# A fused attention and FFN kernel: 256-column halves, two h tiles in one PSUM bank and one pass of 512 columns

## The chip, the cores and the metric

The kernel runs on one core of a Trainium2 chip. The metric is the device time of one execution in microseconds (us). The core has a matrix engine (PE, with its own queue of weight loads, PEld), a vector engine (DVE), a scalar engine (ACT), a general engine (POOL), and queues that issue DMAs (SP and ACT here). Each engine works through its instructions in an order fixed when the kernel is built. [...]

## What is computed

Attention for 8 batches, 8 heads, 576 positions and head size 64, followed by a feed-forward network (512 to 2048 to 512) over all 4608 rows:

```python
cum = np.cumsum(np.maximum(s, 0.0), axis=-1)
bias = -(cum[:, :, :, None] - cum[:, :, None, :])
scores = np.where(causal, -1e9, q @ k.T / sqrt(D) + np.minimum(bias, 0.0))
x = softmax(scores) @ v            # all heads side by side: 4608 x 512
h = x @ w_in                       # 4608 x 2048
g = np.where(h >= 1, h, np.where(h <= -1, 0.0, (h + 1) ** 2 / 4.0))
out = g @ w_out                    # 4608 x 512
```

## The kernel before

Everything is kept transposed: columns are positions, partitions are features. The 576 positions of a batch are cut into two halves (`HALF`): 320 columns (`hf` 0) and 256 columns (`hf` 1). An operand that needs more than fp16 is held as a high and a low fp16 part, so each product takes three matmuls (high-high, low-high, high-low).

**The FFN.** A half has 16 steps, one for each 128 of the 2048 hidden features (`ft` 0 to 15). In a step, `ffn_h` runs 12 matmuls (L530) that sum one h tile into one PSUM bank. The pool `ps_h` has two banks. The activation follows, on three engines in turn: ACT makes u from h (relu with scale and bias, L542), DVE combines h and u (L545), then clips and multiplies (L546), ACT casts the result to fp16 as the high part of g (L556), and POOL subtracts to get the low part (L557). The cast and the subtraction are not issued at once. They wait in `to_split`, and `g_split` issues them behind the relu of the next step (`issue_after(first)`), so that ACT does not stand waiting for DVE.

`ffn_y` runs the 12 matmuls (L569) of one step into four y tiles, one PSUM bank each (tags y0 to y3), that stay open over all 16 steps. At step 15 each y tile is scaled into an SBUF tile `o` (L583 on ACT, L581 on DVE for two tiles of the last half) and written out by DMA (L584). The o tiles take turns in three buffers, the u tiles in four, the g tiles (four steps each) in four.

**The order.** `ffn_step(s, k)` is called with k = 0 (h of step s) and k = 1 (y of an earlier step). y runs `Y_LAG` = 2 steps behind h, over the queue `ffn_q`. The first half of batch 0 is an exception: all 16 h come first, then all y, while the second weight matrix is being prepared.

**Attention beside it.** `att_slot` spreads the attention of the next batch over the same steps: scores on PE (L412, L413; L407 in the first jobs) into the two banks of `ps_s`, a masked minimum on DVE (L418), exp on ACT (L429), the scaled and split weights pb on POOL, ACT and DVE (L450 to L456), a transposing DMA (pt from pb), the product with v on PE (px, L475), and x from it (L486, L487). The 320-column half of the FFN and the 256-column half each have four (head pair, half) jobs of attention beside them, and the jobs need different amounts of work. The last batch's FFN has little or none beside it.

PSUM's eight banks are two of `ps_s`, two of `ps_h` and four of `ps_y`. Which instruction comes first on an engine is chosen by a planner when the kernel is built, from priorities in program order; `high_priority(offset=FFN_LEAD)` moves the activation of the FFN ahead of most attention work, and the masked minimum (`TTR_LEAD`) ahead of that.

Of the kernel before, what the change touches and what calls it, by code (L numbers as in the profile page):

```python
# [9 lines left out]
F32 = mybir.dt.float32  # L10
# [4 lines left out]
AF = mybir.ActivationFunctionType  # L15
ALU = mybir.AluOpType
# [14 lines left out]
HALF = [(0, 320, (0, 1, 2)), (320, 256, (3, 4))]  # L31
# [14 lines left out]
W2_LEAD = 6000  # L46

G_BUFS = 4
O_BUFS = 3
WO_LAG = 2  # L50

Y_LAG = 2

ACT_LOW = {'wi': range(0, 16, 2), 'wo': range(0, 16, 2)}
POOL_LO = {'wi': (8, 12, 13, 14, 15), 'wo': range(16)}
# [16 lines left out]
def attention_ffn(ctx: ExitStack, tc: tile.TileContext, qT, kT, vT, s, w_in, w_out, yT):  # L72
    nc = tc.nc
    LOADQ, CUMQ = nc.sync, nc.scalar
    V, A, G, T = nc.vector, nc.scalar, nc.gpsimd, nc.tensor
# [86 lines left out]
    WI = [cp.tile([P, 2, NC], F16, name=f"WI{c}") for c in range(NW)]  # L162
    WO = [cp.tile([P, 2, NC], F16, name=f"WO{c}") for c in range(NW + WO_LAG)]
# [4 lines left out]
    class Weights:  # L168
# [80 lines left out]
    vraw, csc, rcs, exs, hsc, rsc, usc, wsc, ubi, gsc, ysc, msc = ({} for _ in range(12))  # L249
# [268 lines left out]
            att_out(*jobs[j - 1])  # L518


    ffn_q, g4 = [], [None]

    def ffn_h(b, hf, ft):
        h_off, N, _ = HALF[hf]
        x = X[b, hf]
        h = ps_h.tile([P, 512], F32, tag="h", name=f"h{b}_{hf}_{ft}")
        n = 0
        for kt in range(NKT):
            for wl, xl in ((0, 0), (0, 1), (1, 0)):
                T.matmul(  # L530
                    h[:, :N], WI[4 * kt + ft // 4][:, wl, ft % 4 * P:(ft % 4 + 1) * P], x[:, kt, xl],
                    start=(n == 0), stop=(n == 3 * NKT - 1),
                )
                n += 1
        r, fg = rsc[b], ft // 4
        if ft % 4 == 0:
            g4[0] = gp.tile([P, 4, 2, N], F16, tag="g", bufs=G_BUFS, name=f"g{b}_{hf}_{ft}")
        g = g4[0][:, ft % 4]
        with tc.high_priority(offset=FFN_LEAD):

            u = gp.tile([P, N], F32, tag="u", bufs=4, name=f"u{b}_{hf}_{ft}")
            first = A.activation(u, h[:, :N], AF.Relu, bias=ubi[b], scale=usc[b][:, fg:fg + 1]).ins  # L542

            g_split(first)
            V.scalar_tensor_tensor(h[:, :N], h[:, :N], wsc[b][:, fg:fg + 1], u, ALU.mult, ALU.max)  # L545
            V.scalar_tensor_tensor(u, u, r, h[:, :N], ALU.min, ALU.mult)  # L546
        to_split.append((g, u))
        return g

    to_split = []  # L550

    def g_split(first=None):
        while to_split:
            g, u = to_split.pop()
            with tc.issue_after(first) if first is not None else ExitStack():
                A.copy(g[:, 0], u)  # L556
            G.tensor_tensor(g[:, 1], u, g[:, 0], ALU.subtract)  # L557

    ys = {}

    def ffn_y(b, hf, ft, g, ms=tuple(range(NKT))):
        h_off, N, _ = HALF[hf]
        if ft == 0:
            for m in ms:
                ys[b, hf, m] = ps_y.tile([P, 512], F32, tag=f"y{m}", name=f"y{b}_{hf}_{m}")
        for m in ms:
            c0 = ft % 2 * 2 * P + m % 2 * P
            for n, (wl, gl) in enumerate(((0, 0), (1, 0), (0, 1))):
                T.matmul(  # L569
                    ys[b, hf, m][:, :N], WO[8 * (m // 2) + ft // 2][:, wl, c0:c0 + P], g[:, gl],  # L570
                    start=(ft == 0 and n == 0), stop=(ft == NFT - 1 and n == 2),
                )
        if ft == NFT - 1:
            last = (b, hf) == (B - 1, len(HALF) - 1)
            for m in ms:
                tag, bufs = ("u", 4) if last and m >= 2 else ("o", O_BUFS)
                o = gp.tile([P, N], F32, tag=tag, bufs=bufs, name=f"o{b}_{hf}_{m}")
                y = ys[b, hf, m][:, :N]
                with tc.high_priority(offset=FFN_LEAD):
                    if last and m % 2:  # L580
                        V.tensor_scalar(o, y, ysc[b][m // 2], None, ALU.mult)  # L581
                    else:
                        A.activation(o, y, AF.Copy, scale=ysc[b][m // 2])  # L583
                (nc.sync if last and m % 2 else nc.scalar).dma_start(  # L584
                    yT[m * P:(m + 1) * P, b * S + h_off:b * S + h_off + N], o
                )

    def ffn_step(s, k):

        b, hf, ft = s // (2 * NFT), s // NFT % 2, s % NFT  # L590
        if k == 0:
            ffn_q.append((b, hf, ft, ffn_h(b, hf, ft)))
        elif len(ffn_q) > Y_LAG:
            ffn_y(*ffn_q.pop(0))


    for c in range(3):
# [4 lines left out]
    for j in range(NPAIR):  # L602
        for k in range(8):
            if k % 2 == 0:
                c = 4 * j + k // 2
# [55 lines left out]
    with tc.high_priority(offset=FFN_LEAD):  # L661
        g_split()
    while ffn_q:
        ffn_y(*ffn_q.pop(0))
# [28 lines left out]
```

## Time and profile before

| | |
|---|---|
| three runs | 1110.91, 1114.15, 1114.35 us; median 1114.15 |
| profiled execution | 1111.73 us, of which the span is 1109.9 us |
| mean granted PE clock over the span | 0.963 of full speed |
| h and y matmuls of 320 columns | 1536 each, busy 254.1 and 251.0 us |
| h and y matmuls of 256 columns | 1536 each, busy 209.8 and 206.8 us |
| output DMAs | 32 of 160 KB, 32 of 128 KB |

The span runs from the first instruction to the last; the 1.8 us beside it are around it. Busy time of PE counts a pipelined matmul until its modelled end, so a busy PE need not be at its peak; what is read from the profile is where PE is not busy, and on what it waits. In the rows of the groups, the columns are line, engine, operation, tiles written and read, shapes and count, then busy us in total, mean ns of one, and the idle time of that engine just before such instructions, with what ended most of it. Rows of the timeline give start, length, engine, line and operation. Tile names are the program's own, without buffer numbers: `mn` is the masked minimum, `pb` the split attention weights, `s` a score tile.

### The profile page before, as it was taken

The numbers are of one execution on the slowest core, as the hardware profiler recorded it, in microseconds if no ns is written. First come the engines' busy times: TensorE is split into PE (matmuls) and PEld (weight loads), VectorE is DVE, ScalarE is ACT, GpSimd is POOL, SyncE is SP. The second block draws the span as 40 slices with busy tenths as digits, with TensorE's granted clock in tenths as the row PEclk, the third lists the DMA queues.
The fourth block names the chain that finished last, engine by engine and source line by source line (L and its number), as shares of the span: only waits on it lengthen the run. The fifth ranks groups of instructions, "written<-read, shape, count | busy, mean of one in ns | idle before, by whom it ended". The sixth has DMA issues, their size and how long they took to land.

```text
span 1109.9 us, 25082 instructions
## 1 busy us (share of the span) xinstructions
PE 1010.8 (91%) x8495; PEld 774.9 (70%) x8496; DVE 846.3 (76%) x2325; ACT 725.8 (65%) x1703; POOL 679.0 (61%) x1173
## 2 busy tenths in 40 slices
PE   2456898799999999999999999899999999899998
PEld 1232466587768877777778877687778877787787
DVE  7887966688787877787778877787777887887533
ACT  4765985677567774867567765777576765777432
POOL 4782795775556764766467664666476665765522
PEclk9955999799999999999999999999999999999999
DMA  7876653786468663886468763877387763676300
GB/s 235 218 200 192 170 87 91 158 173 155 100 122 188 148 152 71 187 162 158 79 146 177 161 136 81 177 160 163 68 176 155 165 137 74 158 156 138 68 25 19
DMA packets 340775, 155.01 MB, mean 140 GB/s; under 512 B 290856, under 2 KB 322472, under 8 KB 340648
## 3 DMA queue, kind: packets, MB, share of 16 engines
q1 hardware_dynamic: 330944, 143.49, 59.6%
q10 hardware_dynamic: 9704, 9.93, 2.9%
q8 instruction: 67, 1.10, 0.4%
q14 instruction: 60, 0.49, 0.1%
HBM read 72.31 MB, written 9.73 MB: 74 GB/s over the span
## 4 chain that ended last, share of the span: by engine, by line
PE 61%; DVE 12%; POOL 8%; DMA 7%; issue 6%; ACT 5%; ACTq 0%; SPq 0%; DVEq 0%; POOLq 0%
PE y L569 25%; PE h L530 25%; PE px L475 4%; DMA pt<-pb 3%; PE s L412 3%; PE s L413 3%; DVE pb L456 2%; ACT u L542 2%; POOL pb L453 2%; POOL pb L450 2%; DVE p L418 1%; DVE Q L357 1%; DMA vt<-vb 1%; POOL vb L371 1%; DVE h L545 1%
## 5 line engine op out<-in xcount | busy, mean ns | idle before, releaser
L530 PE MATMUL h<-x,WI 128*128 128x256 f16 (+1 forms) x3072 | 463.9, 290 | 7.4 <-ACT x L486 3.4
L569 PE MATMUL y<-g,WO 128*128 128x256 f16 (+1 forms) x3072 | 457.8, 288 | 7.0 <-POOL g L557 5.3
L530 PEld LDWEIGHTS <-WI 128*128 128x128 f16 x3072 | 291.1, 99 | 97.0 <-issue 13.9
L569 PEld LDWEIGHTS <-WO 128*128 128x128 f16 x3072 | 288.1, 98 | 92.9 <-issue 13.8
L557 POOL TENSOR_TENSOR g<-u,g 128x320 f16<-128x320 f32 (+1 forms) x256 | 206.0, 805 | 152.1 <-ACT g L556 151.6
L429 ACT ACTIVATE p<-p,mn 64x64 f32<-64x64 f32 (+4 forms) x320 | 179.4, 561 | 142.7 <-DVE mn L418 122.2
L542 ACT ACTIVATE u<-h,ub,us 128x320 f32<-128x320 f32 (+1 forms) x256 | 149.1, 583 | 120.3 <-PE h L530 115.3
L545 DVE SCALAR_TENSOR_TENSOR h<-h,ws,u 128x320 f32<-128x320 f32 (+1 forms) x256 | 132.4, 517 | 110.6 <-ACT u L542 108.1
L450 POOL TENSOR_SCALAR pb<-p,rs 64x128 f16<-64x128 f32 (+4 forms) x160 | 95.3, 596 | 171.2 <-DVE rs L446 112.1
L453 POOL TENSOR_TENSOR pb<-p,pb 64x128 f16<-64x128 f32 (+4 forms) x160 | 173.9, 1087 | 9.5
L456 DVE SCALAR_TENSOR_TENSOR pb<-p,rs,pb 64x128 f16<-64x128 f32 (+4 forms) x160 | 134.6, 841 | 47.1 <-POOL pb L450 47.0
L418 DVE CUSTOM_DVE_ANT_0 p<-s,mask 64x64 f32<-64x64 f32 (+4 forms) x320 | 134.4, 420 | 31.3 <-PE s L413 23.0
L412 PE MATMUL s<-K,Q 128*64 128x64 f32 (+1 forms) x336 | 126.2, 377 | 16.0 <-DVE mn L418 10.9
L546 DVE SCALAR_TENSOR_TENSOR u<-u,r,h 128x320 f32<-128x320 f32 (+1 forms) x256 | 130.3, 509 | 6.8 <-DVE h L545 0.5
L451 ACT ACTIVATE p<-p,rs 64x64 f32<-64x64 f32 (+4 forms) x160 | 89.6, 560 | 51.3 <-DVE rs L446 49.4
L556 ACT CAST g<-u 128x320 f16<-128x320 f32 (+1 forms) x256 | 107.9, 421 | 10.3 <-DVE u L546 10.3
L413 PE MATMUL s<-K,Q 68*64 68x64 f32 (+1 forms) x336 | 102.8, 307 | 2.1 <-DMA K<-cumd 1.3
L452 POOL TENSOR_SCALAR pb<-p 64x128 f16<-64x128 f32 (+4 forms) x160 | 93.2, 583 | 11.9 <-ACT p L451 11.0
L475 PEld LDWEIGHTS <-vt 128*64 128x64 f16 x1536 | 73.4, 113 | 36.7 <-issue 30.2
L475 PE MATMUL px<-pt,vt 128*64 128x256 f16 (+3 forms) x1536 | 83.5, 259 | 13.3 <-DMA pt<-pb 8.7
L412 PEld LDWEIGHTS s<-K,Q 128*64 128x64 f32 (+1 forms) x336 | 61.5, 183 | 27.3 <-DVE mn L418 8.2
L413 PEld LDWEIGHTS s<-K,Q 68*64 68x64 f32 (+1 forms) x336 | 61.9, 184 | 5.8 <-issue 1.7
(105 smaller groups left out, 983.0 us busy)
## 6 DMA issues: line engine op xcount, KB each, us to landing
rk<-in_k_dram SPq DMA_DIRECT2D x56, 288.0 KB
v<-in_v_dram SPq DMA_DIRECT2D x32, 288.0 KB
rq<-in_q_dram SPq DMA_DIRECT2D x56, 160.0 KB
rk<-in_k_dram SPq DMA_DIRECT2D x56, 160.0 KB
wir<-in_moe_w_in_dram SPq DMA_DIRECT2D x16, 512.0 KB
wor<-in_moe_w_out_dram SPq DMA_DIRECT2D x16, 512.0 KB
rq<-in_q_dram SPq DMA_DIRECT2D x56, 128.0 KB
out_dram<-o ACTq DMA_DIRECT2D x32, 160.0 KB
```

What stands on the lines that cost most here:

```text
L412: T.matmul(sc[:R, :c1 - c0], Q1[:, hd, qo:qo + R], K1[:, hd, c0:c1], start=True, stop=False)
L413: T.matmul(sc[:R, :c1 - c0], Q2[:KC, hd, qo:qo + R], K2[:KC, hd, c0:c1], start=False, stop=True)
L418: ttr[0] = V.tensor_tensor_reduce(out=Pt[:R, c0:c1], in0=sc[:R, :c1 - c0], in1=mask[:R, mo:mo + c1 - c0], scale=-0.125 if j < F32_JOBS els ...
L429: A.activation(Pt[:R, :W], Pt[:R, :W], AF.Exp, bias=m2[:R], scale=-1.0, accum_out=sums[n, i][:R, hd:hd + 1])
L453: G.tensor_tensor(los[1], pw, his[1], ALU.subtract)
L456: V.scalar_tensor_tensor(los[0], pv, rs[:R, :1], his[0], ALU.mult, ALU.subtract)
L475: T.matmul(px[hd * D:(hd + 1) * D, lo:N], VT[:, vl * NB + j, hd * D:(hd + 1) * D], PT[:, 4 * j + 2 * hd + pl, lo:], start=(m == 0), stop=( ...
L530: T.matmul(h[:, :N], WI[4 * kt + ft // 4][:, wl, ft % 4 * P:(ft % 4 + 1) * P], x[:, kt, xl], start=(n == 0), stop=(n == 3 * NKT - 1),)
L542: first = A.activation(u, h[:, :N], AF.Relu, bias=ubi[b], scale=usc[b][:, fg:fg + 1]).ins
L545: V.scalar_tensor_tensor(h[:, :N], h[:, :N], wsc[b][:, fg:fg + 1], u, ALU.mult, ALU.max)
L557: G.tensor_tensor(g[:, 1], u, g[:, 0], ALU.subtract)
L569: T.matmul(ys[b, hf, m][:, :N], WO[8 * (m // 2) + ft // 2][:, wl, c0:c0 + P], g[:, gl], start=(ft == 0 and n == 0), stop=(ft == NFT - 1 an ...
```

## The change

It concerns the 256-column halves only; what it does to the 320-column halves is to pass through the same code with one tile per bank.

- `ffn_h` puts two consecutive h tiles (even and odd `ft`) side by side into one bank, columns 0 to 255 and 256 to 511. The activation moves to `ffn_g` and runs once for the pair, over 512 columns. The relu thus waits for the matmuls of both tiles.
- `g_split` casts and subtracts the pair in one pass each, behind the relu of the next pair.
- `ffn_y` puts two y tiles into one bank, so that these halves use two of the four y banks. Only the first of the two opens the bank with `start`; `issue_after` keeps the other's opening matmul behind it.
- The output goes out in two tiles of 2 x 256 columns, two DMAs of 256 KB instead of four of 128 KB. These o tiles take turns in the four buffers of u, which grow to 512 columns. In the last half, the second goes over DVE and SP.
- y runs four steps behind h there (`Y_LAG = (2, 4)`). Where a 256-column half begins, two steps run no y; where it ends, two y steps are left to the next half, whose first two steps run two y each.

```diff
-Y_LAG = 2
+Y_LAG = (2, 4)
...
+        c = ft % 2 if hf else 0
+        if c == 0:
+            h2[0] = ps_h.tile([P, 512], F32, tag="h", name=f"h{b}_{hf}_{ft}")
+        h = h2[0]
...
-                    h[:, :N], WI[4 * kt + ft // 4][:, wl, ft % 4 * P:(ft % 4 + 1) * P], x[:, kt, xl],
+                    h[:, c * N:(c + 1) * N], WI[4 * kt + ft // 4][:, wl, ft % 4 * P:(ft % 4 + 1) * P], x[:, kt, xl],
...
+        if hf == 0 or c:
+            ffn_g(b, hf, ft, c + 1)
+        return g4[0][:, ft % 4]
+
+    def ffn_g(b, hf, ft, n):
+        N, r, fg = HALF[hf][1], rsc[b], ft // 4
+        h = h2[0][:, :n * N]
+        g = g4[0][:, ft % 4 + 1 - n:ft % 4 + 1]
         with tc.high_priority(offset=FFN_LEAD):
-            u = gp.tile([P, N], F32, tag="u", bufs=4, name=f"u{b}_{hf}_{ft}")
-            first = A.activation(u, h[:, :N], AF.Relu, bias=ubi[b], scale=usc[b][:, fg:fg + 1]).ins
+            u = gp.tile([P, n * N], F32, tag="u", bufs=U_BUFS, name=f"u{b}_{hf}_{ft}")
+            first = A.activation(u, h, AF.Relu, bias=ubi[b], scale=usc[b][:, fg:fg + 1]).ins
...
-            V.scalar_tensor_tensor(h[:, :N], h[:, :N], wsc[b][:, fg:fg + 1], u, ALU.mult, ALU.max)
-            V.scalar_tensor_tensor(u, u, r, h[:, :N], ALU.min, ALU.mult)
-        to_split.append((g, u))
-        return g
+            V.scalar_tensor_tensor(h, h, wsc[b][:, fg:fg + 1], u, ALU.mult, ALU.max)
+            V.scalar_tensor_tensor(u, u, r, h, ALU.min, ALU.mult)
+        to_split.append((g, u.rearrange("p (f n) -> p f n", f=n)))
...
-                A.copy(g[:, 0], u)
-            G.tensor_tensor(g[:, 1], u, g[:, 0], ALU.subtract)
+                A.copy(g[:, :, 0], u)
+            G.tensor_tensor(g[:, :, 1], u, g[:, :, 0], ALU.subtract)
...
+        w = 1 + hf
         if ft == 0:
             for m in ms:
-                ys[b, hf, m] = ps_y.tile([P, 512], F32, tag=f"y{m}", name=f"y{b}_{hf}_{m}")
+                if m % w == 0:
+                    ys[b, hf, m // w] = ps_y.tile([P, 512], F32, tag=f"y{m // w}", name=f"y{b}_{hf}_{m // w}")
...
+                opens = ft == 0 and n == 0
+                with tc.issue_after(opened[0]) if opens and m % w else ExitStack():
+                    opened[0] = T.matmul(
+                        ys[b, hf, m // w][:, m % w * N:(m % w + 1) * N],
+                        WO[8 * (m // 2) + ft // 2][:, wl, c0:c0 + P], g[:, gl],
+                        start=(opens and m % w == 0), stop=(ft == NFT - 1 and n == 2 and m % w == w - 1),
+                    ).ins
...
-                tag, bufs = ("u", 4) if last and m >= 2 else ("o", O_BUFS)
-                o = gp.tile([P, N], F32, tag=tag, bufs=bufs, name=f"o{b}_{hf}_{m}")
+                tag, bufs = ("u", U_BUFS) if hf else ("o", O_BUFS)
+                o = gp.tile([P, w, N], F32, tag=tag, bufs=bufs, name=f"o{b}_{hf}_{i}")
...
-        elif len(ffn_q) > Y_LAG:
-            ffn_y(*ffn_q.pop(0))
+        else:
+            n = len(ffn_q) - Y_LAG[hf]
+            for _ in range(min(n, 2)):
+                ffn_y(*ffn_q.pop(0))
```

More of the change, by code (lines that the diff above doesn't have):

```diff
@@ L48 @@
 G_BUFS = 4
+U_BUFS = 4
 O_BUFS = 3
 WO_LAG = 2
-Y_LAG = 2
+Y_LAG = (2, 4)
 ACT_LOW = {'wi': range(0, 16, 2), 'wo': range(0, 16, 2)}
@@ L518, in att_slot @@
             att_out(*jobs[j - 1])
-    ffn_q, g4 = [], [None]
+    ffn_q, g4, h2 = [], [None], [None]
     def ffn_h(b, hf, ft):
@@ L525, in ffn_h @@
         x = X[b, hf]
-        h = ps_h.tile([P, 512], F32, tag="h", name=f"h{b}_{hf}_{ft}")
+        c = ft % 2 if hf else 0
+        if c == 0:
+            h2[0] = ps_h.tile([P, 512], F32, tag="h", name=f"h{b}_{hf}_{ft}")
+        h = h2[0]
         n = 0
@@ L534, in ffn_h @@
                 n += 1
-        r, fg = rsc[b], ft // 4
         if ft % 4 == 0:
             g4[0] = gp.tile([P, 4, 2, N], F16, tag="g", bufs=G_BUFS, name=f"g{b}_{hf}_{ft}")
-        g = g4[0][:, ft % 4]
+        if hf == 0 or c:
[5 more added lines that the diff above has]
+        g = g4[0][:, ft % 4 + 1 - n:ft % 4 + 1]
         with tc.high_priority(offset=FFN_LEAD):
-            u = gp.tile([P, N], F32, tag="u", bufs=4, name=f"u{b}_{hf}_{ft}")
-            first = A.activation(u, h[:, :N], AF.Relu, bias=ubi[b], scale=usc[b][:, fg:fg + 1]).ins
+            u = gp.tile([P, n * N], F32, tag="u", bufs=U_BUFS, name=f"u{b}_{hf}_{ft}")
+            first = A.activation(u, h, AF.Relu, bias=ubi[b], scale=usc[b][:, fg:fg + 1]).ins
             g_split(first)
-            V.scalar_tensor_tensor(h[:, :N], h[:, :N], wsc[b][:, fg:fg + 1], u, ALU.mult, ALU.max)
-            V.scalar_tensor_tensor(u, u, r, h[:, :N], ALU.min, ALU.mult)
-        to_split.append((g, u))
-        return g
+            V.scalar_tensor_tensor(h, h, wsc[b][:, fg:fg + 1], u, ALU.mult, ALU.max)
+            V.scalar_tensor_tensor(u, u, r, h, ALU.min, ALU.mult)
+        to_split.append((g, u.rearrange("p (f n) -> p f n", f=n)))
     to_split = []
@@ L555, in g_split @@
             with tc.issue_after(first) if first is not None else ExitStack():
-                A.copy(g[:, 0], u)
-            G.tensor_tensor(g[:, 1], u, g[:, 0], ALU.subtract)
-    ys = {}
+                A.copy(g[:, :, 0], u)
+            G.tensor_tensor(g[:, :, 1], u, g[:, :, 0], ALU.subtract)
+    ys, opened = {}, [None]
     def ffn_y(b, hf, ft, g, ms=tuple(range(NKT))):
         h_off, N, _ = HALF[hf]
+        w = 1 + hf
         if ft == 0:
             for m in ms:
-                ys[b, hf, m] = ps_y.tile([P, 512], F32, tag=f"y{m}", name=f"y{b}_{hf}_{m}")
+                if m % w == 0:
+                    ys[b, hf, m // w] = ps_y.tile([P, 512], F32, tag=f"y{m // w}", name=f"y{b}_{hf}_{m // w}")
         for m in ms:
@@ L568, in ffn_y @@
             for n, (wl, gl) in enumerate(((0, 0), (1, 0), (0, 1))):
[L569 to L572, printed above, removed]
+                opens = ft == 0 and n == 0
[5 more added lines that the diff above has]
+                    ).ins
         if ft == NFT - 1:
             last = (b, hf) == (B - 1, len(HALF) - 1)
-            for m in ms:
-                tag, bufs = ("u", 4) if last and m >= 2 else ("o", O_BUFS)
-                o = gp.tile([P, N], F32, tag=tag, bufs=bufs, name=f"o{b}_{hf}_{m}")
-                y = ys[b, hf, m][:, :N]
+            for i in sorted({m // w for m in ms}):
+                tag, bufs = ("u", U_BUFS) if hf else ("o", O_BUFS)
+                o = gp.tile([P, w, N], F32, tag=tag, bufs=bufs, name=f"o{b}_{hf}_{i}")
+                y = ys[b, hf, i][:, :w * N]
+                on_v = last and i
+                scale = ysc[b][i * w // 2]
                 with tc.high_priority(offset=FFN_LEAD):
-                    if last and m % 2:
-                        V.tensor_scalar(o, y, ysc[b][m // 2], None, ALU.mult)
-                    else:
-                        A.activation(o, y, AF.Copy, scale=ysc[b][m // 2])
-                (nc.sync if last and m % 2 else nc.scalar).dma_start(
-                    yT[m * P:(m + 1) * P, b * S + h_off:b * S + h_off + N], o
+                    if on_v:
+                        V.tensor_scalar(o.rearrange("p m n -> p (m n)"), y, scale, None, ALU.mult)
+                    else:
+                        A.activation(o.rearrange("p m n -> p (m n)"), y, AF.Copy, scale=scale)
+                (nc.sync if on_v else nc.scalar).dma_start(
+                    yT[i * w * P:(i + 1) * w * P, b * S + h_off:b * S + h_off + N].rearrange("(m p) n -> p m n", p=P), o
                 )
```

## The prediction

> **What bounds the kernel now.** The page comes first: the span, the busy shares, the slices and the granted clock.
>
> ```profile
> span 1109.9 us, 25082 instructions
> PE 1010.8 (91%) x8495; PEld 774.9 (70%) x8496; DVE 846.3 (76%) x2325; ACT 725.8 (65%) x1703; POOL 679.0 (61%) x1173
> ...
> PE   2456898799999999999999999899999999899998
> ...
> PEclk9955999799999999999999999999999999999999
> ```
>
> PE is the busiest engine, and nearly every slice (27.7 us) from the ninth on stands at 9, so the start (weights, first batch) holds most of PE's idle time. The change does not touch the start. What matters is whether PE also sets the pace afterwards. So I cut the steady part, from about 250 us, into the halves that the timeline shows: a half begins where h is first written with the other width, as here.
>
> ```profile
> 690.05 0.60 PE L530 MATMUL h<-x,WI 128*128 128x256 f16 x4
> ```
>
> I asked for the busy time of each engine in one 320-column half (first row) and in six 256-column halves (the others). The columns are the stretch, its length, then PE, weight load, DVE, ACT and POOL busy, the clock, and the DMA share.
>
> ```profile
> 627.30:690.00 62.70, 62.70 (x520) 46.65 (x518) 48.68 (x138) 38.03 (x86) 34.85 (x55) 1.00 0.53 114
> ...
> 318.40:381.00 62.60, 59.23 (x551) 49.16 (x550) 51.57 (x151) 47.72 (x127) 44.33 (x94) 0.97 0.81 175
> 444.30:504.40 60.10, 56.60 (x542) 47.38 (x540) 50.07 (x141) 45.61 (x120) 42.28 (x87) 1.00 0.81 172
> 567.20:627.30 60.10, 57.34 (x543) 48.16 (x541) 49.21 (x141) 45.67 (x120) 42.82 (x87) 0.97 0.81 174
> 690.00:751.50 61.50, 56.45 (x543) 47.36 (x542) 49.98 (x141) 45.72 (x120) 41.25 (x87) 1.00 0.81 169
> 814.20:875.30 61.10, 58.41 (x543) 48.44 (x541) 49.23 (x142) 45.94 (x120) 40.48 (x86) 0.97 0.81 167
> 938.00:997.70 59.70, 56.00 (x542) 47.37 (x541) 50.41 (x142) 45.71 (x120) 40.64 (x85) 1.00 0.68 153
> ```
>
> The reader should see a clean split. The 320-column half has no PE idle time: 62.70 of 62.70 us. The 256-column halves, the ones the change edits, leave 62.60-59.23 = 3.37, then 3.50, 2.76, 5.05, 2.69 and 3.70 us: 21.1 us in six halves. Three of them also have a mean clock of 0.97, which is about 0.03 x 61 = 1.8 us each, 5.5 in all. So **26.6 us is the most that relief in these six halves can give.** (The same half of batch 0 lies in the start; that of the last batch has no attention beside it.) The same view in steps of 10 us places the idle time:
>
> ```profile
> 690.00:700.00 10.00, 8.90 (x89) 7.08 (x88) 8.19 (x27) 7.49 (x22) 6.99 (x15) 1.00 0.84 194
> 700.00:710.00 10.00, 8.49 (x86) 7.01 (x85) 7.85 (x26) 8.73 (x27) 6.30 (x18) 1.00 0.89 190
> 710.00:720.00 10.00, 9.03 (x91) 7.69 (x89) 5.85 (x18) 7.10 (x19) 6.35 (x14) 1.00 0.85 142
> 720.00:730.00 10.00, 8.54 (x84) 7.50 (x79) 8.95 (x27) 4.92 (x16) 7.03 (x16) 1.00 0.83 187
> 730.00:740.00 10.00, 10.00 (x97) 8.42 (x96) 9.42 (x25) 8.58 (x21) 6.82 (x15) 1.00 0.63 158
> 740.00:750.00 10.00, 10.00 (x98) 8.43 (x96) 8.23 (x21) 7.40 (x17) 6.27 (x11) 1.00 0.81 132
> ```
>
> PE is short of work only in the first 40 us of the half; the last 20 are full. Who PE waits for, from the view of waits after 250 us (total, times, longest):
>
> ```profile
> PE s L412 <- DVE mn L418: 7.0, 9, 1.9
> PE y L569 <- POOL g L557: 4.9, 6, 1.3
> PE s L412 <- DVE Q L357: 4.2, 5, 1.5
> PE y L569 <- ACT g L556: 1.4, 6, 0.4
> ```
>
> The score matmuls wait for DVE 11.2 us (7.0+4.2), the y matmuls for the g chain 6.3 us (4.9+1.4). The first is attention stuck in DVE's order; the second is the chain that the change rebuilds.
>
> **The change part by part.** *The wider passes.* In a 256-column half the passes over h, u, g and the output go from 256 to 512 columns, and their number halves. No 512-column pass is in the trace, but both widths of before are, and the line through them gives a price.
>
> ```profile
> L557 POOL TENSOR_TENSOR g<-u,g 128x320 f16<-128x320 f32 x128 | 113.0, 883 | 114.3 <-ACT g L556 114.2
> L557 POOL TENSOR_TENSOR g<-u,g 128x256 f16<-128x256 f32 x128 | 92.9, 726 | 37.8 <-ACT g L556 37.4
> L542 ACT ACTIVATE u<-h,ub,us 128x320 f32<-128x320 f32 x128 | 77.9, 609 | 75.3 <-PE h L530 73.0 <-POOL vb L371 1.8 <-POOL p L402 0.2
> ...
> L542 ACT ACTIVATE u<-h,ub,us 128x256 f32<-128x256 f32 x128 | 71.2, 556 | 45.0 <-PE h L530 42.3 <-PE s L413 2.3
> L545 DVE SCALAR_TENSOR_TENSOR h<-h,ws,u 128x320 f32<-128x320 f32 x128 | 70.8, 554 | 77.5 <-ACT u L542 75.2
> L546 DVE SCALAR_TENSOR_TENSOR u<-u,r,h 128x320 f32<-128x320 f32 x128 | 69.3, 542 | 2.7
> L545 DVE SCALAR_TENSOR_TENSOR h<-h,ws,u 128x256 f32<-128x256 f32 x128 | 61.5, 481 | 33.0 <-ACT u L542 32.9
> L546 DVE SCALAR_TENSOR_TENSOR u<-u,r,h 128x256 f32<-128x256 f32 x128 | 60.9, 476 | 4.1 <-DVE h L545 0.5
> L556 ACT CAST g<-u 128x320 f16<-128x320 f32 x128 | 57.4, 448 | 8.6 <-DVE u L546 8.6
> ...
> L556 ACT CAST g<-u 128x256 f16<-128x256 f32 x128 | 50.5, 395 | 1.7 <-DVE u L546 1.7
> ...
> L583 ACT ACTIVATE o<-y,ys 128x320 f32<-128x320 f32 x32 | 15.1, 523 | 8.1 <-PE y L569 7.4 <-DMA out_dram<-o 0.7
> ...
> L583 ACT ACTIVATE o<-y,ys 128x256 f32<-128x256 f32 x30 | 12.5, 468 | 3.8 <-DMA out_dram<-o 2.2 <-PE y L569 1.4
> ```
>
> 64 more columns cost the relu 609-556 = 53 ns, so 256 more cost 212: a 512-column relu is about 768 ns against 2 x 556, 344 saved. In the same way the cast comes to 607 (183 saved), the first DVE pass to 773 (189), the second to 740 (212), the POOL subtraction to 1354 (98), the output copy to 688 (248). Per half, with eight pairs of h and two of output: DVE 8 x 401 = 3.2 us, ACT 8 x 527 + 2 x 248 = 4.7 us, POOL 0.8 us. All this lies beside PE, so its direct worth is nothing; it counts only as far as the queues that PE waits for get shorter.
>
> [...]
>
> *PE's own work* does not change: 3072 h and 3072 y matmuls at the same widths, only into the other half of a bank. Nothing is gained there. Nor is there a reason for loss: the opening order of two output tiles (issue_after) binds PE's own order only.
>
> *The g chain and the lag.* The cast of a pair is queued on ACT behind the relu of the next pair. So y of an even step ft has to wait for h of ft+3, then relu, cast and POOL: 768+607+1354 = 2.73 us, where it was h of ft+1 and 556+395+726 = 1.68 us. In program order y(ft-1) and h(ft+4) lie between, as y(ft-1) and h(ft+2) did: the same cover, a chain 1.05 us longer. But each odd step finds its g ready with its partner's, and PE can run h ahead over two banks of two tiles instead of two of one. Between the ends, all 6.3 us gone and each of the 12 waits above 1.05 us longer (+12.6), I take half gone: **-3.1 us.** Queued behind a late cast on ACT are the exps, and behind a late subtraction on POOL the pb products of attention.
>
> *DVE's queue.* By the middle of a half, where the stalls lie, four pairs have freed 1.6 us on DVE, about as much as a half's waits for DVE (11.2 / 6 = 1.9). Against it stands grain: an attention step that arrives behind a pass waits up to 773 instead of 481 ns. Between none and all of 11.2 I take half: **-5.6 us**. [...]
>
> ```profile
> 568.49 1.25 PE L569 MATMUL y<-g,WO 128*128 128x320 f16 x8
> ...
> 575.33 0.33 PE L412 MATMUL s<-K,Q 128*128 128x192 f32 x1 [1.95 <-DVE mn L418]
> ...
> 577.00 2.29 PE L569 MATMUL y<-g,WO 128*128 128x320 f16 x8 [0.15 <-ACT g L556]
> ```
>
> The same eight y take 1.25 us before and 2.29 after a wait of 1.95. I take one of the three such windows as gone, **-1.8 us** (ends 0 and -5.5). [...]
>
> *Work moved between halves.* With a lag of four, the first two steps of a 256-column half run no y, and two y steps of it run in the next 320-column half, which has no idle time. Their size, from the chain of waits:
>
> ```profile
> 340.06 1.31 PE h L530 x12
> ```
>
> A y step is the same 12 matmuls of this width. Two are 2.62 us a half, 18.3 over seven halves that have attention beside them, if the half they leave gets no shorter; nothing, if PE sets its length. The last 20 us of the half (10.00 of 10.00) speak for nothing, the thin first 20 for something: I take **+4 us**, nearer to nothing.
>
> *Outputs and the end.* The outputs of these halves now use the ring of four u buffers. Before, the ring of three made ACT wait for output DMAs 3.0 us in all (row below); I take nothing, between -2.2 us (the part that the 256-column copies waited) and +3.0. ACT issues 15 output DMAs of 256 KB for 30 of 128 KB; those issues run on its queue beside its passes, so nothing.
>
> ```profile
> ACT o L583 <- DMA out_dram<-o: 3.0, 3, 1.2
> ```
>
> At the end of the kernel:
>
> ```profile
> 1105.83 0.88 DVE L581 TENSOR_SCALAR o<-y,ys 128x256 f32<-128x256 f32 x2 [1.98 <-PE y L569]
> ```
>
> The last copy doubles in width, and its DMA in size, after PE's last matmul: **+0.5 us**, between 0.3 and 1.
>
> **Sum:** -3.1 - 5.6 - 1.8 + 4 + 0.5 = -6.0 us. The profiled execution took 1111.73 us, so 1105.7, given as **1106**. The three runs' median is 1114.15 and their lowest 1110.91; a measurement of this kernel tells about 0.3% (3.3 us) from no change.
>
> **The rivals.** *Large relief:* the wider look-ahead clears nearly all stalls of the six halves, up to 26.6 us: 1085 to 1098, say 1092. For it: the stalls are few and tied to DVE and g. Against it: L412 waits for steps of attention whose own inputs the change does not touch. *No effect:* the score stalls are latency of attention, not load on DVE; the freed 3.2 us become DVE idle time, and what y gains the longer chain takes back: 1111, within 3.3 us of before. For it: in 710 to 720 PE idles with DVE at only 5.85 of 10. *Slower by lost cover:* the place is the first 20 us of each 256-column half. Attention is dense there, and PE is left with h alone for two steps. If attention sets the length of these halves, each 320-column half grows by 2.62 us and nothing shrinks: up to 1111.7 + 18.3 = 1130, half of it 1121. It decides once the y taken out exceed what the half's PE time falls short of, that is, if the 256-column halves stay at 60 us while the 320-column halves go from 62.7 to 65.
>
> **How the numbers follow.** Forecast (3.5 to 14 us gained) 0.40; large relief 0.14; no effect 0.22; lost cover 0.24. Faster by over 0.3% is 0.40 + 0.14 = 0.54, within 0.22, slower 0.24. The range, 1093 to 1121, leaves out about half of the large relief (0.07) and under half of lost cover (0.11). Since both signs hold much of the chance: the forecast's own range is 1098 to 1108.
>
> **What would show it.** Right: the 256-column halves have PE idle of 1 to 2.5 us instead of 3.5, DVE busy there about 46.9 instead of 50.1 us (the mean of the six rows), the 512-column relu at 0.77 us, and the 320-column halves stay full, longer by at most the 2.6 us that the 256-column ones lose. The lag is wrong if y still waits 5 us or more for POOL's g; the DVE step is wrong if DVE's busy time falls and the score waits stay at 11 us. The whole is wrong if stalls appear in the 320-column halves, where u buffers shared with outputs or a late g would show.

## The result and the profile after

The changed kernel takes 1123.38 us (median of 15 runs) against 1114.35 us (median of 15): **0.8% slower**, ratio 1.008 with a 95% interval of 1.0061 to 1.0098. The profiled execution took 1123.41 us against 1111.73, the span 1121.6 against 1109.9: 11.7 us more. The ratios here and below leave out three executions far above the others of their kernel (2067.5 us before, 1203.19 us changed, 1331.45 us for the kernel before with attention further ahead). The page of the changed kernel, span and busy times:

```profile
span 1121.6 us, 24629 instructions
...
PE 1010.9 (90%) x8496; PEld 774.0 (69%) x8496; DVE 853.9 (76%) x2196; ACT 700.8 (62%) x1560; POOL 672.0 (60%) x1109
```

PE's work is unchanged (1010.9 against 1010.8 us), ACT has lost 25 us, POOL 7, and DVE has *gained* 7.6, although its passes became cheaper. So the 11.7 us are time in which PE is idle: 9.3 of them lie between 250 and 1060 us (30.5 us of idle time instead of 21.2), 1.6 behind that and 0.7 ahead of it. The halves of the changed kernel, cut where h changes its width, first three of 320 columns (length, then PE, weight load, DVE, ACT, POOL busy, clock):

```profile
501.60:572.20 70.60, 68.42 (x568) 50.61 (x567) 55.32 (x144) 42.50 (x91) 39.02 (x60) 1.00 0.59 120
626.30:696.30 70.00, 68.30 (x569) 50.57 (x567) 55.72 (x144) 42.55 (x91) 38.92 (x59) 1.00 0.60 121
750.80:821.60 70.80, 68.26 (x569) 50.76 (x568) 54.72 (x144) 42.41 (x92) 39.75 (x60) 1.00 0.55 121
```

and then three of 256 columns:

```profile
572.20:626.30 54.10, 51.44 (x495) 43.45 (x494) 45.02 (x118) 38.31 (x97) 37.75 (x74) 1.00 0.77 167
696.30:750.80 54.50, 51.38 (x494) 43.50 (x492) 44.59 (x118) 38.35 (x97) 37.79 (x74) 1.00 0.79 167
821.60:874.40 52.80, 51.15 (x493) 43.37 (x492) 44.43 (x118) 38.19 (x97) 37.58 (x74) 1.00 0.78 169
```

With two banks of two h tiles, h runs ahead: a 256-column half, counted from h, is 54 us instead of 61, and the next one 70 instead of 63. The 320-column half has lost its perfect cover: 70.00-68.30 = 1.70 us idle, 2.18 and 2.54 beside it, where there was none. The 256-column halves still idle (2.66, 3.12, 1.65). Stalls in the 320-column halves are the sign that the prediction named for its whole being wrong. Who PE waits for in the same stretch as before, 250 to 1060 us (the largest rows: total, times, longest):

```profile
PE px L476 <- DMA pt<-pb: 6.7, 8, 2.2
PE s L413 <- DVE mn L419: 3.8, 7, 1.1
PE y L581 <- POOL g L565: 3.8, 7, 1.0
PE h L534 <- DVE u L555: 3.7, 6, 1.1
PE s L413 <- DVE Q L358: 3.7, 6, 1.6
PE y L581 <- ACT g L564: 3.2, 5, 0.7
```

All rows of this view together are 29.3 us, and 20.5 before. The score matmuls do wait less for DVE (3.8+3.7 = 7.5 instead of 11.2). In their place stand px waiting for the transposing DMA of pb (6.7, before 0.8), h waiting for DVE to empty its bank (3.7, before none there), and y waiting for ACT's cast (3.2, before 1.4).

### The profile page after: what moved, and what is told of

Same layout as the page of the kernel before. It is cut to its first block, busy times and chain, and to the rows that moved or that the text cites. A ratio compares the mean times of both kernels' runs of the same rounds, so it can differ in the third digit from the quotient of the medians.

```text
span 1121.6 us, 24629 instructions
## 1 busy us (share of the span) xinstructions
PE 1010.9 (90%) x8496; PEld 774.0 (69%) x8496; DVE 853.9 (76%) x2196; ACT 700.8 (62%) x1560; POOL 672.0 (60%) x1109
## 4 chain that ended last, share of the span: by engine, by line
PE 46%; DVE 20%; DMA 7%; issue 7%; ACT 6%; POOL 5%; ACTq 0%; POOLq 0%; DVEq 0%
PE y L581 19%; PE h L534 18%; DMA pt<-pb 5%; DVE pb L457 4%; PE px L476 4%; DVE p L419 3%; DVE h L554 3%; DVE u L555 2%; PE s L413 2%; ACT p L430 2%; POOL pb L451 2%; PE s L414 2%; DVE K L361 2%; DVE Q L358 1%; DVE c L261 1%
## 5 line engine op out<-in xcount | busy, mean ns | idle before, releaser
L581 PE MATMUL y<-g,WO 128*128 128x256 f16 (+1 forms) x3072 | 447.5, 288 | 7.8 <-POOL g L565 4.4
L565 POOL TENSOR_TENSOR g<-u,g 128x320 f16<-128x320 f32 (+1 forms) x192 | 187.5, 977 | 137.9 <-ACT g L564 137.5
L551 ACT ACTIVATE u<-h,ub,us 128x320 f32<-128x320 f32 (+1 forms) x192 | 126.6, 660 | 117.5 <-PE h L534 117.0
L457 DVE SCALAR_TENSOR_TENSOR pb<-p,rs,pb 64x128 f16<-64x128 f32 (+4 forms) x160 | 152.3, 952 | 49.8 <-POOL pb L451 49.6
L554 DVE SCALAR_TENSOR_TENSOR h<-h,ws,u 128x320 f32<-128x320 f32 (+1 forms) x192 | 118.7, 619 | 85.6 <-ACT u L551 83.6
L454 POOL TENSOR_TENSOR pb<-p,pb 64x128 f16<-64x128 f32 (+4 forms) x160 | 167.3, 1046 | 9.0
L555 DVE SCALAR_TENSOR_TENSOR u<-u,r,h 128x320 f32<-128x320 f32 (+1 forms) x192 | 116.6, 608 | 4.2
L564 ACT CAST g<-u 128x320 f16<-128x320 f32 (+1 forms) x192 | 96.1, 500 | 15.5 <-DVE u L555 15.5
L453 POOL TENSOR_SCALAR pb<-p 64x128 f16<-64x128 f32 (+4 forms) x160 | 101.6, 635 | 5.4 <-ACT p L452 4.2
L361 DVE TENSOR_TENSOR K<-rk,K 64x1152 fp32r<-64x1152 f32 (+1 forms) x52 | 62.9, 1210 | 4.6 <-ACT K L356 3.5
```

Of the source, the lines that this page charges most:

```text
L454: G.tensor_tensor(los[1], pw, his[1], ALU.subtract)
L457: V.scalar_tensor_tensor(los[0], pv, rs[:R, :1], his[0], ALU.mult, ALU.subtract)
L551: first = A.activation(u, h, AF.Relu, bias=ubi[b], scale=usc[b][:, fg:fg + 1]).ins
L554: V.scalar_tensor_tensor(h, h, wsc[b][:, fg:fg + 1], u, ALU.mult, ALU.max)
L555: V.scalar_tensor_tensor(u, u, r, h, ALU.min, ALU.mult)
L565: G.tensor_tensor(g[:, :, 1], u, g[:, :, 0], ALU.subtract)
```

## The experiments

Four theories were open. **L**, lost cover: the lag of four takes y away from the start of the 256-column half, where it filled a stall. **W**, width: a 512-column pass holds DVE, ACT and POOL longer at a time (rows of 607 to 1160 ns after, of 395 to 726 for the 256-column passes before). **P**, the pair: its chain through h's bank, relu, cast and POOL makes new waits in whatever order. **N**, the order: the planner lays out every engine's instructions anew after any edit, and a new order moves the time by as much as the change did. In a later group **O** asks what the paired outputs give. Ratios are to the kernel before in runs of the same chip.

### Taking the change apart

The lag alone, on the kernel before:

```diff
-Y_LAG = 2
+Y_LAG = (2, 4)
...
-        elif len(ffn_q) > Y_LAG:
-            ffn_y(*ffn_q.pop(0))
+        else:
+            n = len(ffn_q) - Y_LAG[hf]
+            for _ in range(min(n, 2)):
+                ffn_y(*ffn_q.pop(0))
```

> The kernel before with one edit: y runs four steps behind h in the 256-column halves (two y a step while it catches up); tiles, passes, banks and outputs stay 256 wide. Theory L (lost cover: the two y steps moved out of each 256-column half cost the time): +6 to +12 us against before, as the changed kernel (+9). Theory W (the 512-column passes hold DVE, ACT and POOL longer at a time) and theory P (the pair makes h and y wait for each other's bank and the g chain): within 3 us of before, since nothing is paired.

The change with a lag of three:

```diff
-Y_LAG = (2, 4)
+Y_LAG = (2, 3)
```

> The changed kernel with the lag of 3 instead of 4 in the 256-column halves (the least that the pair allows, since the cast of a pair is issued behind the relu of the next). Theory L: only one y step is moved out, so about half of the loss comes back, +4 to +6 us against before. Theory W and P: as the changed kernel, +8 to +10 us, or worse, since y of an even step now has no cover step left (P: y waits for g of 5 us and more beyond the 7.0 us of the changed kernel).

The pair with two narrow passes:

```diff
-            ffn_g(b, hf, ft, c + 1)
+            for d in range(c, -1, -1):
+                ffn_g(b, hf, ft - d, c - d)
...
-        h = h2[0][:, :n * N]
-        g = g4[0][:, ft % 4 + 1 - n:ft % 4 + 1]
+        n = 1
+        h = h2[0][:, c * N:(c + 1) * N]
+        g = g4[0][:, ft % 4:ft % 4 + 1]
```

> The changed kernel, but the relu, both DVE passes, the cast and the POOL subtraction of a pair run as two of 256 columns each, after both tiles are summed; pair, banks, lag and outputs stay as changed. Theory W: back to within 3 us of before, and pb on DVE back to about 841 ns from 952. Theory L and P: as the changed kernel or slower, +9 to +13 us, since DVE and ACT have the fixed costs back (3.2 and 4.2 us a half).

Only h paired:

```diff
-        w = 1 + hf
+        w = 1
...
-                tag, bufs = ("u", U_BUFS) if hf else ("o", O_BUFS)
+                tag, bufs = ("u", U_BUFS) if last and i >= 2 else ("o", O_BUFS)
...
-                on_v = last and i
-                scale = ysc[b][i * w // 2]
+                on_v = last and i % 2
+                scale = ysc[b][i // 2]
```

> The changed kernel with h paired and passes of 512 columns and the lag of 4, but y in four banks and four outputs of 256 columns in the ring of o, as before. If the y pairs and the outputs in the ring of u cost something (theory O): 3 us or more faster than the changed kernel. Theories L, W and P: as the changed kernel, +7 to +11 us against before.

| run | median us | ratio (95%) |
|---|---|---|
| lag alone | 1122.07 | 1.0071 (1.0053 to 1.0089) |
| change, lag 3 | 1136.34 | 1.0215 (1.0193 to 1.0237) |
| change, narrow passes | 1133.44 | 1.0185 (1.0166 to 1.0205) |
| only h paired | 1138.54 | 1.0222 (1.0191 to 1.0253) |

W's forecast failed: with narrow passes the kernel is 10 us slower than with wide ones, and pb on DVE, which I had expected back at 841 ns, took 893. That does not rule out a cost of width: differences of 10 us come from the order too, as later runs show, and the section on the prediction finds one such cost in the traces. The lag alone does what L said, and the trace shows where. The timeline of PE in the kernel before, from the px product that opens the 256-column half to the score matmul that waits:

```profile
692.53 1.51 PE L475 MATMUL px<-pt,vt 128*64 128x256 f16 x30
...
694.70 0.45 PE L569 MATMUL y<-g,WO 128*128 128x320 f16 x2
694.98 1.36 PE L530 MATMUL h<-x,WI 128*128 128x256 f16 x11
...
697.17 0.33 PE L412 MATMUL s<-K,Q 128*128 128x192 f32 x1 [0.74 <-DVE mn L418]
```

and the same place with the lag alone:

```profile
700.92 1.51 PE L475 MATMUL px<-pt,vt 128*64 128x256 f16 x30
...
702.74 0.57 PE L569 MATMUL y<-g,WO 128*128 128x320 f16 x3
...
703.24 0.40 PE L530 MATMUL h<-x,WI 128*128 128x256 f16 x2
705.54 0.33 PE L412 MATMUL s<-K,Q 128*128 128x192 f32 x1 [1.91 <-DVE mn L418]
```

The score matmul becomes free 4.6 us after px began in both (697.17-692.53, 705.54-700.92): DVE sets that moment. What differs is how much PE has to do until then, and the wait grows from 0.74 to 1.91 us. In the view of waits, s for DVE's mn rises from 7.0 to 13.6 us: six waits of 1.9 to 2.7 us, one at this place of each 256-column half.

The other two fit less. With a lag of three, y waits 10.9 us in the view of waits instead of 7.0, the direction that P had, though 3.9 us more and not the 5 or more that it asked for. But the scores' wait for DVE grows as well, from 7.5 to 17.8, and half of L's loss does not come back. And pairing h alone costs 25 us, and pairing y and the outputs as well gives 15 of them back, which no term of the sum can explain. And the lag alone, with nothing paired, costs as much as the whole change (1.0071 and 1.0080), but by other waits: the changed kernel has 3.8 us of s for mn, all in the first 12 us of 320-column halves, where the lag alone has 13.6.

### Is it the part or the order?

The kernel before with `Y_LAG = 4` in both halves, so that no half starts without y:

> The kernel before with y four steps behind h in both halves, nothing paired: every step from the fifth on has one y, so no half begins with steps that run no y. Theory L (the lag of four costs because y is missing at the start of the 256-column half, where a score matmul waits for DVE after px; 13.6 us of that wait with the lag alone, 7.0 before): the wait is back to about 7 us and the time within 3 us of before. Rival K (a lag of four costs by itself, h too far ahead holding u and g buffers, or another order): +5 to +10 us as with the lag alone.

The changed kernel with `Y_LAG = (4, 4)`:

> The changed kernel with a lag of four in both halves. Theory L: 5 to 9 us faster than the changed kernel, near before (1110 to 1118 us). Theory P (the longer chain of the pair through wide passes sets new waits wherever it stands: h for DVE, y for ACT's and POOL's g, 11 us together in the changed kernel): within 3 us of the changed kernel, about 1123.

Only y and the outputs paired, h not, lag 2:

```diff
-Y_LAG = (2, 4)
+Y_LAG = (2, 2)
...
-        c = ft % 2 if hf else 0
+        c = 0
...
-        if hf == 0 or c:
+        if True:
```

> The kernel before with only the y tiles paired in banks and the outputs as two tiles of 512 columns in the ring of u; h and its passes 256 wide, lag 2. Theory O (paired outputs are worth the 15 us by which the changed kernel beat the one with only h paired): 3 to 15 us faster than before. Rival N (that difference was an accident of the order that the planner chose): within 4 us of before.

And a shift of the order with no other edit, on the kernel before:

```diff
-FFN_LEAD = 6000
+FFN_LEAD = 7000
```

> The kernel before with one number of the planner's priorities changed (FFN_LEAD 7000 instead of 6000): the same instructions and tiles, another static order on every engine. Rival N (differences of some 10 us come from the order alone, whatever the edit): 5 us or more away from before, on either side. Theories L, P and O need it within 3 us of before, so that their own differences mean something.

| run | median us | ratio (95%) |
|---|---|---|
| before, lag 4 and 4 | 1114.42 | 1.0015 (0.9996 to 1.0034) |
| change, lag 4 and 4 | 1127.61 | 1.0134 (1.0105 to 1.0163) |
| only y paired, lag 2 | 1121.52 | 1.0075 (1.0050 to 1.0100) |
| before, other priority | 1120.92 | 1.0070 (1.0045 to 1.0095) |

L holds for the kernel before: with y in every step the wait of s for mn is 7.6 us and the loss is gone. It does not hold for the changed kernel, which gets no faster. O's forecast of a gain failed: the paired outputs alone are 0.7% slower. And one number of the planner's priorities, with the same instructions, costs 7.9 us: nearly what the change cost. That asks for the same comparison in other orders.

### The change in other orders

v is turned (transposed by DMA) one attention slot later (`V_K = 6` for 5), in both kernels; and attention is called further ahead (the extra slots go on until step 8 * NFT instead of 6 * NFT, which makes four more), in both:

> The kernel before with v of the next job turned one attention slot later (V_K 6 instead of 5): same work, another static order throughout. Rival N (the time hangs on the order by some 8 us, as one change of priorities showed, and the kernel before sits in a good order): 4 to 12 us slower than before. Theory P: within 4 us of before.

> The changed kernel with the same shift (V_K 6). Rival N: no rule against its partner with V_K 6; the two lie within 5 us of each other, or the changed one is the faster. Theory P (pairing costs by its longer chain in whatever order): 5 to 15 us slower than its partner.

> The kernel before with attention ahead of the FFN by two more slots (the extra slot goes on until step 128 instead of 96): same work, another order and another offset of attention against the halves. Rival N: 4 to 15 us away from before. Theory P: within 4 us of before.

> The changed kernel with the same offset. Rival N: within 5 us of its partner with this offset, on either side. Theory P: 5 to 15 us slower than its partner.

| order | before's side | changed side |
|---|---|---|
| V_K 6 | 1129.93, 1.0153 (1.0123 to 1.0184) | 1118.26, 1.0059 (1.0038 to 1.0081) |
| attention further ahead | 1113.05, 1.0006 (0.9983 to 1.0028) | 1122.51, 1.0099 (1.0071 to 1.0127) |

With V_K 6 the sign turns round: the changed side is 11.7 us *faster* than its partner. The two profiled spans, 1131.5 and 1116.6 us, are 14.9 us apart, and most of that is PE itself. Its busy time with V_K 6, first of the unchanged tiles, then of the changed ones:

```profile
PE 1022.1 (90%) x8495; PEld 778.6 (69%) x8496; DVE 866.6 (77%) x2325; ACT 727.0 (64%) x1703; POOL 678.4 (60%) x1173
...
PE 1010.9 (91%) x8495; PEld 773.6 (69%) x8496; DVE 846.5 (76%) x2196; ACT 703.6 (63%) x1560; POOL 665.7 (60%) x1109
```

The same matmuls keep PE busy 11.2 us longer on before's side, where the mean granted clock over the span is 0.975 and not 0.988. PE's waits differ by 3.8 us (29.4 and 25.6). The largest rows of the unchanged tiles:

```profile
PE s L412 <- DVE mn L418: 11.7, 11, 2.8
PE y L569 <- POOL g L557: 6.5, 9, 3.0
```

and of the changed ones:

```profile
PE s L413 <- DVE mn L419: 9.9, 14, 1.4
PE y L581 <- ACT g L564: 3.9, 6, 0.6
PE h L534 <- DVE u L555: 3.7, 6, 0.8
```

The kernel before catches long waits there for scores (up to 2.8 us) and for POOL's g (up to 3.0), and the changed one does not, with no wait over 1.4 us; its px for the DMA of pb, the largest row without the shift, falls to 1.4 us in all. Whether the long waits and the lower clock belong together, no run shows.

The second shift is no other order. In the trace of before's side, PE, DVE and POOL run their instructions in exactly the sequence of before, compared by tile and shape, and DVE and POOL do so on the changed side too. So N's forecasts for this pair were not put to the test. The pair repeats the first measurement, with before unmoved (1.0006) and a difference of 9 us.

### Taking the paired waits away

Two waits recur in the five kernels so far with h paired, wide passes and a lag of four: in all of them y for ACT's cast (3.2 to 3.9 us) at the end of a 256-column half, where the last pair's cast is queued behind the next half's first relu, and in three h for DVE's u (3.6 to 3.7). ACT and then PE at the end of one such half:

```profile
382.45 0.62 ACT L551 ACTIVATE u<-h,ub,us 128x320 f32<-128x320 f32 x1 [1.14 <-PE h L534]
382.96 0.60 ACT L564 CAST g<-u 128x512 f16<-128x512 f32 x1
...
383.62 0.60 PE L581 MATMUL y<-g,WO 128*128 128x256 f16 x4 [0.66 <-ACT g L564]
```

The second comes behind four reductions over v that DVE runs in one piece. The timeline of DVE after:

```profile
668.92 2.72 DVE L261 TENSOR_REDUCE c<-v 128x1 f32<-128x576 f32 x4
671.57 0.55 DVE L554 SCALAR_TENSOR_TENSOR h<-h,ws,u 128x320 f32<-128x320 f32 x1
```

and of PE:

```profile
673.14 1.79 PE L534 MATMUL h<-x,WI 128*128 128x320 f16 x12 [0.62 <-DVE u L555]
```

The kernel before has the same block, and PE waits for nothing there:

```profile
663.10 2.72 DVE L260 TENSOR_REDUCE c<-v 128x1 f32<-128x576 f32 x4
```

The edit for the first wait, alone and with V_K 6:

```diff
         to_split.append((g, u.rearrange("p (f n) -> p f n", f=n)))
+        if hf and ft == NFT - 1:
+            with tc.high_priority(offset=FFN_LEAD):
+                g_split()
```

> The changed kernel, but the cast and the subtraction of the last pair of each 256-column half are issued at once and no longer behind the first relu of the next half. Theory P (the pair's g chain makes y wait at the end of each half for ACT's cast, 3.2 us in all and about 0.65 us in the last half): that wait falls under 1.5 us and the kernel is 2 to 4 us faster than the changed one. Rival N (order alone): the wait may go, but the time moves by 5 us or more on either side, with other waits.

> The changed kernel with v turned one slot later (1118.3 us) and the last pair issued at once. Theory P: the y wait for ACT's cast goes from 3.9 us to under 1.5, 2 to 4 us faster than with the later turn alone, 1114 to 1116. Rival N: 5 us or more away on either side.

The edit for the second, on the changed kernel and, as a control, on the one before (`batch_v` keeps the reductions of the first batch alone):

```diff
+    def batch_c(b, p):
+        if p == 0:
+            csc[b] = ap.tile([P, NPAIR], F32, tag="csc", name=f"c{b}")
+        V.tensor_reduce(csc[b][:, p:p + 1], vraw[b, p], axis=AX, op=ALU.max, apply_absolute_value=True)
...
+            if last_job and 2 <= k <= 5:
+                with tc.issue_after(ttr[0]):
+                    batch_c(jobs[j + 1][0] // NPAIR, k - 2)
```

> The changed kernel with the four reductions over v of the next batch issued in four attention slots instead of back to back (2.7 us of DVE in one piece, behind which the passes over h stood). Theory P with this place: the wait of h for DVE's u falls from 3.7 us to under 1 and the kernel is 3 to 4 us faster than the changed one, about 1119. Rival N: the time moves by 5 us or more on either side.

> The kernel before with the same spread of the four reductions. It has no wait of h for DVE in the steady part, so theory P expects no change, within 3 us of before. Rival N: 4 to 15 us slower, as the other shifts of order made it.

Then the control for the first, the same three lines in the kernel before, and both edits together in the changed one:

> The kernel before with the cast and the subtraction of the last step of each 256-column half issued at once. Theory P: y waits there for ACT's cast only 0.2 us a half, so nothing to gain, within 3 us of before. Rival N: 4 to 15 us away, most likely slower.

> The changed kernel with both edits: last pair issued at once, reductions spread. Theory P: the two gains add where they remove different waits (h for u is already at 0.5 us with the first alone), so 1106 to 1111. Rival N: a new order, 1110 to 1125.

| run | median us | ratio (95%) | PE's waits, 250 to 1060 us |
|---|---|---|---|
| before (profiled 1111.73) | 1114.35 | 1 | 20.5 |
| changed (profiled 1123.41) | 1123.38 | 1.0080 (1.0061 to 1.0098) | 29.3 |
| last pair at once | 1110.25 | **0.9969** (0.9954 to 0.9985) | 16.5 |
| the same with V_K 6 | 1116.34 | 1.0034 (1.0016 to 1.0051) | 23.2 |
| reductions spread | 1114.11 | 1.0012 (0.9985 to 1.0039) | 22.0 |
| before, reductions spread | 1122.48 | 1.0073 (1.0045 to 1.0101) | 26.2 |
| before, last step at once | 1112.07 | 0.9991 (0.9974 to 1.0009) | 18.9 |
| changed, both edits | 1132.84 | 1.0168 (1.0139 to 1.0196) | 34.5 |

Each edit alone removes the wait it aims at (y for ACT's cast from 3.2 to none, h for u from 3.7 to 0.8), and each gives back far more than that wait: by the ratios 1.1% and 0.7%, about 12 and 8 us. Together, they are the slowest of the group, slower than either theory allowed. With V_K 6 the first edit does not even remove its wait (3.1 us are left), though the time falls by about what P said. In the kernel before, the spread costs 0.7% where P expected nothing. The last step at once changes nothing there, as P said and N did not; PE's sequence hardly moved either (96% of its neighbouring pairs of instructions are those of before, 86% with V_K 6).

So neither theory holds throughout. N is right in that orders with the same instructions lie up to 1.5% apart and turn the sign; it does not say when they do. P is right about where two of the waits stand, and wrong about what they are worth. The waits of the best one, the last pair issued at once:

```profile
PE s L414 <- DMA K<-cumd: 9.4, 6, 2.7
PE px L476 <- DMA pt<-pb: 1.7, 3, 0.8
```

y waits for nothing there, and scores hardly for DVE; one DMA is left. And those of both edits together:

```profile
PE s L419 <- DVE Q L364: 11.3, 9, 2.5
PE y L594 <- POOL g L578: 8.0, 8, 1.7
```

The stalls are back, at other places. A line through all 20 profiled executions gives the time as 1088 us and 1.28 us for each us of these waits (correlation 0.94): what sets a kernel of this family apart is, for the most part, how long PE stands in front of instructions whose inputs are late. That is close to bookkeeping, since the matmuls are the same in all of them; it does not say why an order has its waits. Part of the rest is PE's own busy time: 1010.8 us before and 1022.1 with V_K 6, for the same matmuls.

## Why the prediction was wrong

**The reading of the bound was right.** PE's own work did not change, and the whole loss is PE's idle time: the rows of the wait view show 8.8 us more (29.3-20.5), out of 11.7.

**The prices of the passes were right**, but for POOL's. The rows of the 512-column passes after:

```profile
L565 POOL TENSOR_TENSOR g<-u,g 128x512 f16<-128x512 f32 x64 | 74.2, 1160 | 33.5 <-ACT g L564 33.4
L551 ACT ACTIVATE u<-h,ub,us 128x512 f32<-128x512 f32 x64 | 49.0, 766 | 35.7 <-PE h L534 35.5
L554 DVE SCALAR_TENSOR_TENSOR h<-h,ws,u 128x512 f32<-128x512 f32 x64 | 48.0, 749 | 32.3 <-ACT u L551 32.2
L555 DVE SCALAR_TENSOR_TENSOR u<-u,r,h 128x512 f32<-128x512 f32 x64 | 47.3, 739 | 1.2
L564 ACT CAST g<-u 128x512 f16<-128x512 f32 x64 | 38.9, 607 | 1.7 <-DVE u L555 1.7
L598 ACT ACTIVATE o<-y,ys 128x512 f32<-128x512 f32 x15 | 10.2, 679 | 6.4 <-PE y L581 6.4
```

766, 749, 739, 607 and 679 ns stand against 768, 773, 740, 607 and 688; only POOL's subtraction, at 1160, undercut its 1354, by 14%.

**The relief of DVE did not stay.** The two DVE passes shed 27 us, and DVE's busy time rose by 7.6. The largest part of what ate it is pb, before:

```profile
L456 DVE SCALAR_TENSOR_TENSOR pb<-p,rs,pb 64x128 f16<-64x128 f32 (+4 forms) x160 | 134.6, 841 | 47.1 <-POOL pb L450 47.0
```

after:

```profile
L457 DVE SCALAR_TENSOR_TENSOR pb<-p,rs,pb 64x128 f16<-64x128 f32 (+4 forms) x160 | 152.3, 952 | 49.8 <-POOL pb L451 49.6
```

and with the last pair issued at once:

```profile
L457 DVE SCALAR_TENSOR_TENSOR pb<-p,rs,pb 64x128 f16<-64x128 f32 (+4 forms) x160 | 133.4, 834 | 32.1 <-POOL pb L451 31.0 <-POOL pb L453 0.3
```

The same 160 instructions on the same data cost 952 or 834 ns on average, with the same wide passes in the kernel. The timelines of DVE and POOL after show beside what they are slow:

```profile
488.88 0.48 DVE L457 SCALAR_TENSOR_TENSOR pb<-p,rs,pb 128x256 f16<-128x256 f32 x1 [1.12 <-POOL pb L451]
...
589.00 1.15 POOL L565 TENSOR_TENSOR g<-u,g 128x512 f16<-128x512 f32 x1
589.07 1.37 DVE L457 SCALAR_TENSOR_TENSOR pb<-p,rs,pb 128x256 f16<-128x256 f32 x1 [1.11 <-POOL pb L451]
```

At 488.88 us POOL is idle, and at 589.07 its 512-column subtraction has just begun. Of the 32 pb passes of this shape, 11 start beside the wide subtraction after and take 1.26 to 1.37 us; beside the narrow one they take 0.68 to 0.88 us, before and after, and without POOL under 0.5. So this is a cost of the wider pass, which the sum did not have because all passes were priced alone. That the order decides how often it is paid is my reading of the two means, 952 and 834 ns. How much of it reaches PE, by a later transposing DMA of pb, no run shows.

**The term for DVE's queue** (-5.6) had the right sign, by luck as far as its reason goes: the scores wait 3.7 us less for DVE, but DVE was not relieved. **The term for the clock** (-1.8) came out larger than forecast in what it counts, a mean clock under full speed in one half of the changed kernel (0.98 in one of 72.7 us) instead of three (0.97); but PE's busy time from 250 us on did not fall (835.5 us, before 834.8), so the gain is not to be seen in the time. That a slow window goes with its stall was my estimate, and no run shows it. **The end** (+0.5) came out at +0.6, from the start of DVE's first output copy to the end of the span (1109.9-1105.83 = 4.07, now 1121.6-1116.93 = 4.67), but a second cost at the end was missed: the last pair's chain is longer than its cover.

```profile
1111.86 4.96 PE L581 MATMUL y<-g,WO 128*128 128x256 f16 x44 [0.63 <-POOL g L565]
...
1116.93 0.75 DVE L596 TENSOR_SCALAR o<-y,ys 128x512 f32<-128x512 f32 x1 [5.22 <-PE y L581]
```

**The step that failed first is the g chain and the lag**, "I take half gone: -3.1 us". y waits 7.0 us instead of 3.2 (6.3-3.1), and that is 0.7 more than before where 3.1 less was forecast. I had worked out that the chain of an even step is 1.05 us longer and then let the look-ahead outweigh it; at the end of each half, where the cast stands behind the relu of another half, it did not. ACT's cast went from 1.4 to 3.2 us, POOL's g from 4.9 to 3.8.

**The step that failed for good lies under all the others.** The sum takes the waits of before as places that stay, and subtracts from them. They do not stay. px for the transposing DMA (+5.9) and h for DVE (+3.7) are in no term, because before neither had been late (0.8 us and none). Shifts that change no instruction moved the kernel before by +0.7% (another priority), +0.7% (reductions spread) and +1.5% (V_K 6), all upwards; the lag of four in both halves (+0.2%) and the last step at once (-0.1%) left it within their intervals of no change. In pairs of kernels that share the shift, the change costs +0.8% (as given, +0.9% when repeated), +1.2% (lag of four in both), +0.1% (lag of two and four in both, the lag alone as partner), -0.9% (V_K 6), -0.6% (reductions spread) and -0.2% (last pair at once; the intervals of the two overlap). A forecast of -0.5% for one of them cannot be had by subtracting waits, and a range of 1093 to 1121 was too narrow for the 1110 to 1139 that these edits of the changed kernel cover.

**The rival on the slower side** named the right danger at the wrong address. Lost cover at the start of the 256-column half is real and costs 8 us, twice the term of +4, but in the kernel without pairs; in the changed one no score waits for mn at that place, and a lag without the gap (four and four) does not help it. What the +4 came to in the changed kernel cannot be taken out of its time. Its sign, 256-column halves that stay at 60 us, did not appear either: they shrank to 54.

What stays open: how much of the 9 us is the pair's own. The waits for the cast and for u (3.2 and 3.7 us) are argued from the traces to belong to it; that their removal brought about 12 and 8 us shows that the rest came with the order. Whether some order favours the kernel before in the same way, beyond the one it has, was not searched. The best version found is the changed kernel with the last pair issued at once: 0.3% faster than before (0.9969) and 1.1% faster than the change as given (0.9969 against 1.0080), in one order.

## What to carry to other kernels

Where one engine is full and its order is fixed in advance, price an edit in two parts: the work it saves, which rows gave to about 3% for five of six passes here (14% off for POOL's), and the new order, which they do not give. A pass also slowed what ran beside it, which its own row does not show: pb of 256 columns took 1.26 to 1.37 us beside the wide subtraction, 0.68 to 0.88 beside the narrow one. Before believing a difference of 1%, make the same comparison under two or three shifts that change no work (a priority, a slot), and see in the traces that each shift did move the order; here that turned the sign. Filler in front of a late instruction hid its stall here: the same late score matmul cost 0.74 us with eleven matmuls of h ahead of it and 1.91 with two.

## What was not expected of the hardware

In the kernel before, a stretch at half the clock (0.50 between 576.60 and 580.00 us) came behind a wait of 1.95 us, the longest from 250 to 1060 us. In the changed kernel the longest wait there is 2.24 us, in front of px at 960.37 us. The stretches of 3.4 us around it (length, then PE, weight load, DVE, ACT, POOL busy, clock) stay at full speed, while three waits of 0.66, 0.67 and 0.30 us between 383 and 386 us are followed by 0.54:

```profile
383.40:386.80 3.40, 2.21 (x14) 1.49 (x14) 3.40 (x10) 2.70 (x8) 1.67 (x5) 0.96 0.91 194
386.80:390.20 3.40, 3.40 (x18) 2.42 (x17) 1.99 (x7) 1.97 (x4) 1.38 (x2) 0.54 0.63 119
...
957.00:960.40 3.40, 1.16 (x11) 0.65 (x9) 3.34 (x7) 2.84 (x7) 0.00 (x0) 1.00 1.01 157
960.40:963.80 3.40, 3.40 (x42) 3.12 (x43) 0.58 (x2) 2.87 (x8) 1.97 (x4) 1.00 0.69 177
```

PE was busy for 2.21 of 3.40 us ahead of the stretch at 0.54 and for 1.16 of 3.40 ahead of one that stayed at 1.00. So at these two places the idle time of the stretch ahead did not tell by itself whether the clock would fall; no run here shows what makes it fall.
